# Attention, mixture of experts and a gated feed-forward stage on one core: register loads of the second half's tiles placed later, last-stage weight loads queued at another point

## The chip, the cores and the metric

One core of a Trainium2 chip runs the whole program. The metric is the device time of one execution in microseconds (us). The kernel before took 522.54 us (median of three runs: 522.54, 524.20, 521.99). The trace comes from one more, profiled execution, of 523.88 us.

The engines are TensorE (PE in the profile; its weight loads are PEld), VectorE (DVE), ScalarE (ACT), GpSimd (POOL) and SyncE (SP). SP computes nothing here: it issues most of the DMAs, one after the other. Every engine works through its own list of instructions in order; where an instruction waits, all behind it in that list wait too.

## The reference

```python
x = attention(q, k, v)                    # 2 x 8 heads, 576 rows of 64, rotary embedding, softmax
x = x.transpose(0, 2, 1, 3).reshape(1152, 512)
e = argmax(x @ w_gate + bias[modality])   # one of 8 experts for each token, gate weight = its probability
out[mask_e] = gate * (relu(x[mask_e] @ w1[e]) @ w2[e])      # w1[e] 512 x 1024, w2[e] 1024 x 512
h = out @ w_in                            # 512 x 2048
y = (h * tanh(softplus(h))) @ w_out       # 2048 x 512
```

Everything is float32. A product is made of three passes on TensorE: each operand is split into a rounded high part and the rest (names in `h` and `l`, as `whi` and `wlo`), and high x high, high x low and low x high are added in PSUM.

## The kernel before, in words

**Stages.** Attention takes the first 170 us. Then come the experts: the tokens of each half of the batch are sorted by expert into rows of a scratch tensor in HBM, and the work is cut into tiles of 304 rows of one expert. Four tiles are always done, named (0, 0), (0, 1), (1, 0) and (1, 1): half and number. Any tile beyond these is done in a loop `For_i(0, n_extra)`, whose count `n_extra` is found on the chip; here it is passed without a turn. From 303 us on runs the last stage, the feed-forward part (`h_unit`, `o_unit` and the `g_` functions).

**One tile.** A tile reads its rows (`xrow`), transposes them (L661), and runs 8 groups of 12 matmuls for the first matrix (`f` in `moe_tile`, whi/wlo chunks 0 to 3, two groups a chunk) and 4 groups of 24 for the second (`d`, chunks 4 to 7). Each of the 8 weight chunks of 512 KB is loaded by SP (`wraw`, L590), rounded on ACT (`whi`, L598) and subtracted on POOL (`wlo`, L603; two of them on DVE). The groups' results pass through ACT (`hh`, L718) and DVE (`hl`, L720).

**Routing of half 1.** While tile (0, 0) starts, DVE works out where the tokens of half 1 go: a chain of some forty small instructions in `routing(1)` and `merge_extra`. Matmuls of tile (0, 0) are put between them by `pump`: each DVE step gives a credit from `P["rq"]`, which is spent on matmuls. The chain leaves three things: the table `tbl` with expert and row of tiles (1, 0) and (1, 1), the list `extra` of further tiles, and their number `nxi`. `tile_rows(1)` has SP read `tbl` into registers (`value_load`, L554 and L555). `values_load(nx)` (L1378) has all five engines read `nxi` into a register.

**Weights of the last stage.** Its 16 weight blocks of 1 MB come in as 64-bit words (`wr`, loaded by `dec_load`, L1289) and are turned into float32 by three DVE instructions a block (L1296, L1301, L1306; `decode` runs one of them). There are two `wr` buffers, so block f + 2 can be loaded only when the third instruction of block f is done. `decode` is called by `drive` at every 24th matmul step of the expert stage, and 48 such instructions are spread over expert and last stage; those that are left when the last stage begins are put between its own DVE work.

Of the kernel before, what the change touches and what calls it, by code (L numbers as in the profile page):

```python
# [35 lines left out]
FC2 = F2 // 128  # L36

Q = {'r0': 2.45, 'rd': 2.0, 'tanh': 1.06, 'rec': 1.1, 'hi': 2.2, 'lo': 2.38, 'o': 3.86}
P = {'sd': (3, 4), 'dl': (28, 44), 'qd': (2, 3), 'alt': (0.1, 4), 'd0': 41, 'vl': 9, 'w3': 3, 'rq': (0.45, 0.47, 0.2), 'dec': (8, 8, 8), 'rl': 3, 'ah': 0, 'eps': 0.05, 'slack': 0.1}
K = {'ld': -22.67, 'prep': (-24.92, -22.38, -23.33, -27.14, -20.49, -7.62), 'sc': (-8.42, -3.18, 1.68, 1.67, 2.84, 10.44, 1.99, 8.05, 9.75), 'max': (-2.26, -5.46, -1.21, -1.85, 5.06, 8.41, 4.71, 11.42, 13.72), 'exp': (-3.19, 1.66, 6.32, 3.7, 13.26, 11.14, 14.6, -2.87, 25.74), 'tr': (0.69, 2.1, 2.56, 2.68, 5.53, 7.5, 8.45, 9.85, 10.88, 11.85, 15.56, 16.66, 16.92, 19.98), 'hi': (-3.91, -0.31, 2.51, 3.62, 4.25, 4.9, 5.01, 5.32, 7.26, 9.77, 13.56, 14.12, 14.6, 15.66), 'lo': (0.77, 1.83, 5.61, 6.34, 6.67, 7.32, 10.02, 10.73, 12.18, 13.92, 13.94, 14.62, 17.33, 18.02), 'pv': (7.08, 7.84, 10.5, 10.69, 14.13, 14.25, 14.32, 15.96, 18.04, 20.31, 21.03, 22.86, 23.97, 25.61), 'evac': (14.53, 9.65, 6.27, 25.13), 'rec': (-4.7, -0.45, 4.11, 12.71), 'fmm': (4.53, -3.79, 16.24, 17.22), 'norm': (15.5, 16.11, 26.18, 35.69)}  # L40

QT = [(0, 128), (128, 128), (256, 64), (320, 128), (448, 128)]
# [31 lines left out]
class Plan:  # L74
# [39 lines left out]
    def pick(self, e):  # L114
        best, lines = None, set()
        for o in self.todo[e][:40]:
# [8 lines left out]
            if best is None or t < best[0] - 1e-9:  # L125
                best = (t, o)
            if t <= self.free[e] + P["eps"]:
                break
# [40 lines left out]
    def run(self):  # L169
# [3 lines left out]
        while any(self.todo.values()):  # L173
            best = None
            for e in self.todo:
                c = self.pick(e)
                c = c and (c[0], 1, c[1])
                for o in self.alt[e][:4]:
# [4 lines left out]
                    t = max(t, self.free[e])  # L183
                    if (c is None or t + o[4] - P["alt"][0] <= c[0]) and t + o[4] + P["alt"][1] < end:
                        c = (t, 1, o)
                for st in self.streams:
# [3 lines left out]
                    if st["gate"] and not st["gate"](t):  # L190
                        continue
                    if c is None or t + (st["next"][1] - P["slack"] if e in st["low"] else 0.0) <= c[0]:
                        c = (t, 0, st)
# [19 lines left out]
def moe_kernel(ctx: ExitStack, tc: tile.TileContext, aps, out):  # L213
    nc = tc.nc
    scratch = nc.dram_tensor("scratch", [ROWS, RW], F32).ap()
    extra = nc.dram_tensor("extra", [NS[1] - 2, 2], I32).ap()
# [309 lines left out]
    def merge_extra(nx):  # L526

        V = nc.vector
        n0, n1 = NS[0] - 2, NS[1] - 2
        sh = [1, n0, 2]  # L530
        m = rp.tile([1, n0], F32, tag="mm", name="mm")
        yield "dve", 0.12, True
        V.tensor_scalar(
            out=m, in0=iotat[0:1, 0:n0], scalar1=nxs[0], scalar2=None, op0=ALU.is_lt
        )
        d = rp.tile(sh, F32, tag="md", name="md")
        yield "dve", 0.12, True
        V.tensor_tensor(out=d, in0=tes[0][:, 2:], in1=tms[1][:, 2:2 + n0], op=ALU.subtract)
        yield "dve", 0.12, True
        V.tensor_tensor(out=d, in0=d, in1=m[:, :, None].to_broadcast(sh), op=ALU.mult)  # L540
        yield "dve", 0.12, True
        V.tensor_tensor(
            out=tes[1][:, 2:2 + n0], in0=tms[1][:, 2:2 + n0], in1=d, op=ALU.add
        )
        ei = const.tile([1, n1, 2], I32, name="ei")
        yield "dve", 0.12, True
        V.tensor_copy(ei, tes[1][:, 2:])
        yield "dve", 0.12, True
        V.tensor_tensor(out=nx, in0=nxs[0], in1=nxs[1], op=ALU.add)
        nc.sync.dma_start(out=extra.rearrange("(o r) c -> o r c", o=1), in_=ei)  # L550

    def tile_regs(row):
        return dict(
            e=nc.sync.value_load(row[:, 0:1], min_val=0, max_val=NE - 1),  # L554
            c=nc.sync.value_load(row[:, 1:2], min_val=0, max_val=ROWS - T),  # L555
            y=lambda: nc.scalar.value_load(row[:, 1:2], min_val=0, max_val=ROWS - T),
        )
# [34 lines left out]
    def split_chunk(k, i):  # L592
# [6 lines left out]
        lo = pool.tile([128, 1024], F32R, tag="wlo", name=f"wlo{k}_{i}", bufs=n)  # L599
        dve = k == (0, 0) and i in P["sd"]  # L600
        yield ("dve", 1.14, False) if dve else ("pool", 2.3, False)
# [4 lines left out]
    class Feed:  # L606
# [6 lines left out]
        def loads(self, n):  # L613
            self.want = max(self.want, min(n, len(self.seq)))
            while self.nl < min(self.want, self.ns + (2 if len(wpool) == 1 else P["w3"])):
                k = self.seq[self.nl][0]
# [56 lines left out]
    def moe_tile(k, feed, bank):  # L673

        at_ = feed.tiles.index(k)
        ah = 4 if len(wpool) == 1 else 2 + P["w3"] + P["ah"]
        kk = at_ * NCH
# [516 lines left out]
    cur = {}  # L1194

    def all_tiles(keys):
        for k in keys:
            yield from moe_tile(k, feed, lambda: cur["bank"]())

    gen0 = all_tiles(main[:2])  # L1200
    done0 = []

    def route(b):
        yield from routing(b, lambda: cur["rbank"]())
        if b:
            tile_rows(b)

    def tile_rows(b):
        for i in range(2):
            regs[b, i] = tile_regs(tbl[b][:, i])  # L1210
# [52 lines left out]
    def pump(x):  # L1263

        owed[0] += x
        while owed[0] > 0:
            y = next(gen0, None)
            if y is None:
                done0.append(1)
                return  # L1270
            if y[0] == "pe":
                owed[0] -= y[1]
# [14 lines left out]
    def dec_load(f):  # L1287
        wr[f] = t = wrp.tile([128, 1024, 2], I32, tag="wr", name=f"wr{f}")
        nc.sync.dma_start(out=t.rearrange("p a b -> p (a b)"), in_=aps["wio"][f].bitcast(I32))  # L1289

    def dec(f):


        t = wr.pop(f)
        w = WC[f].bitcast(I32)
        nc.vector.tensor_scalar(  # L1296
            out=w, in0=t[:, :, 1], scalar1=3, scalar2=0x3FFFFFFF,
            op0=ALU.logical_shift_left, op1=ALU.bitwise_and,
        )
        yield  # L1300
        nc.vector.scalar_tensor_tensor(  # L1301
            out=w, in0=t[:, :, 1], scalar=-0x40000000, in1=w,
            op0=ALU.bitwise_and, op1=ALU.bitwise_or,
        )
        yield
        nc.vector.scalar_tensor_tensor(  # L1306
            out=w, in0=t[:, :, 0], scalar=29, in1=w,
            op0=ALU.logical_shift_right, op1=ALU.bitwise_or,
        )
        yield  # L1310

    def dec_all():
        for f in range(FC2):
            d = dec(f)
            next(d)
            yield
            next(d)
            yield
            next(d)
            if f + 2 < FC2:  # L1320
                dec_load(f + 2)
            yield

    dgen = dec_all()
    nd = [0]

    def decode(n, limit=3 * FC2):
        for _ in range(n):
            if nd[0] < limit:
                nd[0] += 1  # L1330
                next(dgen)

    with ExitStack() as mctx:
# [11 lines left out]
        nq_ = [0]  # L1345

        def drive(gen, every, limit=3 * FC2, steps=1000):
            for y in gen:
                if y == "last":
                    break  # L1350
                if y == "quiet":
                    limit = 0
                if y[0] == "y":
                    for i in range(2):
                        split_y(0, i, y[1:])
                if y[0] != "pe":
                    continue
                nq_[0] += 1
                if nq_[0] % (3 * every) == 0:
                    decode(1, limit)  # L1360
                steps -= 1
                if not steps:
                    break
# [3 lines left out]
        for i, y in enumerate(chain(route(1), merge_extra(nx))):  # L1367
            if i in P["dl"]:
                dec_load(len(wr))
            if y[0] == "dve":  # L1370
                pump(P["rq"][(i > 9) + (i > 20)])
        xctx.close()
        lctx = ExitStack()
        for c, n, b in ((sctx, "wp3", P["w3"]), (lctx, "lp", 1)):
# [17 lines left out]
        def split_y(g, i, cs=range(KC)):  # L1392
            c0, n, hs = GR[g]
            o, w = T + c0 + sum(hs[:i]), hs[i]
            if cs[0] == 0:
                yh[g, i] = ypool[g].tile([128, KC, w], F32R, name=f"yh{g}_{i}")
                yl[g, i] = ypool[g].tile([128, KC, w], F32R, name=f"yl{g}_{i}")
            a, b = yh[g, i], yl[g, i]
            for c in cs:
                nc.scalar.activation(out=a[:, c], in_=Y[:, c, o:o + w], func=AF.Copy)  # L1400
                nc.vector.tensor_tensor(  # L1401
                    out=b[:, c], in0=Y[:, c, o:o + w], in1=a[:, c].bitcast(F32), op=ALU.subtract
                )
# [141 lines left out]
        for q in range(nq):  # L1545
# [18 lines left out]
            o = m + Q["o"]  # L1564
# [17 lines left out]
        ps_h = pool("ps_h", 3, space=PSUM)  # L1582
        for i in range(2):
            split_y(0, i, [KC - 1])
        for _, _, fn, a in sorted(ev2, key=lambda e: e[:2]):
            fn(*a)

# [58 lines left out]
```

## Time and profile before

| | |
|---|---|
| median of three runs | 522.54 us |
| profiled execution | 523.88 us, of it 522.2 us from the first to the last instruction |
| PE busy | 480.7 us (92% of the span) |
| DVE, POOL, ACT busy | 409.8, 366.3, 332.4 us |
| mean granted TensorE clock | 0.977 of full speed |

A busy share is a mean over stages that have different limits. To judge one place one looks at the stretch of the span it lies in: what each engine did there, what PE waited for, and which clock it was granted. Matmuls overlap, so the time of one matmul is read from the distance between starts or from a long run of them, not from a single duration.

### The profile page before, as it was taken

To read this page: it belongs to the slowest core of one execution; us is meant where nothing else is said; L and a number is where in the kernel's file an instruction comes from. 1 tells how busy PE (TensorE), PEld (TensorE's weight loads), DVE (VectorE), ACT (ScalarE), POOL (GpSimd) and SP (SyncE) were. 2 spreads that over 40 slices of the span, in tenths; PEclk is the share of its full clock that TensorE was granted. 3 is DMA by queue.
4 is the path that set the end of the run, shared out by engine and by line. 5 is a ranking of instruction groups with operands and counts; after the bars stand their busy time and mean duration, and the time that the engine had idled before them with its cause. 6 is when DMAs were issued, how large, how long until landed. Compare 5 with 4: busy or idle time off the path is not lost.

```text
span 522.2 us, 9092 instructions
## 1 busy us (share of the span) xinstructions
PE 480.7 (92%) x3152; PEld 444.8 (85%) x3152; DVE 409.8 (78%) x586; ACT 332.4 (64%) x750; POOL 366.3 (70%) x359
## 2 busy tenths in 40 slices
PE   2699999999999979898999988899999899999995
PEld 1589999998988869897989987789898789999994
DVE  6489888898887665481696889999999967877773
ACT  2388788767869515454464475666666568776763
POOL 4889989999833355664777665677778558977664
PEclk9999999999999979899999999999999899999998
DMA  6588976777633684683875522022220000100001
GB/s 210 140 193 228 229 204 171 208 185 206 140 122 130 203 313 158 225 310 121 282 247 203 211 82 81 1 81 82 80 82 2 1 2 40 49 14 1 1 1 81
DMA packets 24131, 69.42 MB, mean 133 GB/s; under 512 B 5522, under 2 KB 9810, under 8 KB 22034
## 3 DMA queue, kind: packets, MB, share of 16 engines
q1 hardware_dynamic: 21794, 63.16, 39.9%
q0 software_dynamic: 1456, 5.03, 2.4%
q10 hardware_dynamic: 832, 0.61, 0.4%
q8 instruction: 26, 0.43, 0.3%
q14 instruction: 23, 0.19, 0.1%
HBM read 49.08 MB, written 6.44 MB: 106 GB/s over the span
## 4 chain that ended last, share of the span: by engine, by line
PE 34%; DVE 12%; ACT 2%; issue 2%; POOL 2%; DMA 1%; POOLq 0%; ACTq 0%
PE h L1453 13%; PE o L1510 13%; PE mm L695 7%; DVE ta L1475 6%; DVE wc L1306 1%; DVE wc L1301 1%; DMA wraw(1, 0)_5_3587<-in_w_dram 1%; DVE yl L1401 1%; DVE ta L1476 1%; POOL wlo(1, 0)_2_3552 L603 1%; POOL wlo(1, 0)_1_3542 L603 0%; ACT w2h L1436 0%; PE mm L661 0%; DVE wc L1296 0%; POOL out_dram L1520 0%
## 5 line engine op out<-in xcount | busy, mean ns | idle before, releaser
L1475 DVE RECIPROCAL ta<-ta 128x320 f32<-128x320 f32 (+1 forms) x64 | 124.7, 1948 | 22.0 <-ACT ta L1468 20.7
L1493 POOL TENSOR_TENSOR g<-ta,g 128x320 fp32r<-128x320 f32 (+1 forms) x63 | 60.1, 954 | 61.4 <-issue 29.0
L1510 PE MATMUL o<-w2h,g 128*128 128x512 f32 x288 | 101.0, 398 | 0.0
L1437 POOL TENSOR_TENSOR w2l<-wc,w2h 128x512 fp32r<-128x512 f32 x64 | 85.7, 1360 | 3.5 <-ACT w2h L1436 3.5
L1453 PE MATMUL h<-yh,w2h 128*128 128x320 f32 (+1 forms) x256 | 76.4, 299 | 6.2 <-DVE ta L1476 6.2
L1453 PE MATMUL h<-yh,w2l 128*128 128x320 f32 (+1 forms) x256 | 76.2, 298 | 0.6 <-POOL w2l L1437 0.6
L1453 PE MATMUL h<-yl,w2h 128*128 128x320 f32 (+1 forms) x256 | 75.9, 297 | 0.2 <-DVE yl L1401 0.2
L963 PE MATMUL sc<-sk,sq 128*128 128x288 f32 (+1 forms) x320 | 59.8, 320 | 15.4 <-ACT sk L890 9.4
L984 ACT ACTIVATE pexp<-sc,nm 128x576 f32<-128x576 f32 x72 | 53.3, 741 | 24.2 <-DVE nm L973 19.3
L973 DVE TENSOR_REDUCE nm<-sc 128x1 f32<-128x576 f32 x72 | 53.5, 751 | 14.6 <-PE sc L963 11.0
L1510 PEld LDWEIGHTS o<-w2h,g 128*128 128x128 f32 x288 | 54.5, 190 | 11.0 <-POOL g L1493 1.0
L963 PEld LDWEIGHTS sc<-sk,sq 128*128 128x128 f32 (+1 forms) x320 | 47.6, 195 | 17.7 <-ACT sk L890 9.4
L1017 ACT ACTIVATE ph<-pt 128x512 fp32r<-128x512 f32 (+2 forms) x112 | 54.6, 510 | 12.2 <-PE pt L997 11.6
L1453 PEld LDWEIGHTS h<-yh,w2h 128*128 128x128 f32 x256 | 48.4, 189 | 11.1 <-DVE ta L1476 7.8
L997 PE MATMUL pt<-ident,pexp 128*128 128x128 f32 (+1 forms) x360 | 54.9, 278 | 2.7 <-DVE pl L1023 1.8
L1510 PE MATMUL o<-w2l,g 128*128 128x512 f32 x144 | 57.2, 397 | 0.0
L1487 ACT ACTIVATE g<-ta 128x320 fp32r<-128x320 f32 (+1 forms) x64 | 27.9, 436 | 41.7 <-DVE ta L1476 41.6
L1023 DVE TENSOR_TENSOR pl<-pt,ph 128x512 fp32r<-128x512 f32 (+1 forms) x80 | 48.9, 628 | 3.0 <-ACT ph L1017 2.6
L1038 PE MATMUL av<-ph,vhl 128*128 128x256 f32 (+1 forms) x160 | 50.9, 334 | 0.4 <-ACT avt L1047 0.2
L1453 PEld LDWEIGHTS h<-yl,w2h 128*128 128x128 f32 x256 | 48.3, 189 | 2.6 <-DVE yl L1401 0.4
L1453 PEld LDWEIGHTS h<-yh,w2l 128*128 128x128 f32 x256 | 48.3, 189 | 0.8 <-POOL w2l L1437 0.8
L997 PEld LDWEIGHTS pt<-ident,pexp 128*128 128x128 f32 (+1 forms) x360 | 42.1, 138 | 5.7 <-issue 2.0
(440 smaller groups left out, 1229.5 us busy)
## 6 DMA issues: line engine op xcount, KB each, us to landing
wr<-in_wio_dram SPq DMA_DIRECT2D x16, 1024.0 KB, 4.8
xs<-in_qk_dram SPq DMA_DIRECT2D x15, 576.0 KB, 5.1
sk<-ab SPq DMA_DIRECT2D x30, 288.0 KB, 4.1
sq<-ab SPq DMA_DIRECT2D x30, 144.0 KB, 2.6
vraw<-in_v_dram SPq DMA_DIRECT2D x16, 160.0 KB, 3.9
scratch<-zero SPq DMA_DIRECT2D x12, 108.8 KB, 3.8
xrow(0, 0)_2307<-scratch SPq DMA_DIRECT2D x2, 290.0 KB, 2.9
xrow(0, 1)_2675<-scratch SPq DMA_DIRECT2D x2, 290.0 KB, 4.2
```

The costliest lines, as they stand in the source:

```text
L963: nc.tensor.matmul(t[:m, hf, :NC2], lhsT=sq[:, c:c + m], rhs=sk[:, z, hf * NC2:(hf + 1) * NC2], start=(z == 0), stop=(z == 1),)
L973: nc.vector.tensor_reduce(out=nm[n, j], in_=sc[n, j][:, :, :NC2], axis=AX.XY, op=ALU.max, negate=True)
L984: nc.scalar.activation(out=pe, in_=sc.pop((n, j))[:, :, :NC2], func=AF.Exp, bias=nm.pop((n, j)), accum_out=st[n, hf][:, i:i + 1],)
L997: nc.tensor.transpose(out=t[:kn, o:o + 128], in_=pexp[n, j][:, k0:k0 + kn], identity=ident)
L1017: nc.scalar.activation(out=block(ph, n, hf, kts, slice(0, kn)), in_=psum(n, hf, kts, kn), func=AF.Copy)
L1023: nc.vector.tensor_tensor(out=block(pl, n, hf, kts, slice(0, 128)) if kn == 128 else block(ph, n, hf, kts, slice(64, 128)), in0=psum(n, hf ...
L1038: nc.tensor.matmul(av[n, hf][:, :u.nq], lhsT=vhl[n][:, kt].rearrange("p a d -> p (a d)"), rhs=src[:, kt, u.at:u.at + u.nq], start=(kt == 0 ...
L1437: nc.gpsimd.tensor_tensor(out=lo[:, cs], in0=w[:, cs], in1=hi[:, cs].bitcast(F32), op=ALU.subtract)
L1453: nc.tensor.matmul(ps[:, :w], lhsT=wt[:, c], rhs=m[g, i][:, c], start=(n == 0), stop=(n == 11))
L1475: nc.vector.reciprocal(out=ta, in_=ta)
L1493: eng.tensor_tensor(out=gt[q][1][:, o:o + w], in0=tas.pop((q, i))[:, :w], in1=gt[q][0][:, o:o + w].bitcast(F32), op=ALU.subtract,)
L1510: nc.tensor.matmul(acc[g, t], lhsT=a[:, s], rhs=b, start=(f == 0 and z == 0), stop=(f == FC2 - 1 and z == 2),)
```

## The change

Four things are altered.

- The credits of `pump` go from (0.45, 0.47, 0.2) to (0.52, 0.55, 0.25).
- After the routing chain, 24 further matmul steps of the expert tiles are issued before `tile_rows(1)`, and the DMA of `extra` is issued there too instead of at the end of `merge_extra`.
- After them another 24 steps (9 before) come ahead of `values_load(nx)`.
- `dec_all` no longer issues the next `wr` load right behind the third decoding instruction. It notes it in `due`, and `flush` issues it 16 matmul steps later. From the last stage on it is issued at once, as before.

```diff
-P = {... 'vl': 9, 'w3': 3, 'rq': (0.45, 0.47, 0.2), ...}
+P = {... 'vl': 24, 'w3': 3, 'rq': (0.52, 0.55, 0.25), ...}
...
-        nc.sync.dma_start(out=extra.rearrange("(o r) c -> o r c", o=1), in_=ei)
+        cur["ei"] = ei
...
     def route(b):
         yield from routing(b, lambda: cur["rbank"]())
-        if b:
-            tile_rows(b)
...
+    due, behind = [], [True]
+
+    def flush():
+        while due:
+            dec_load(due.pop(0))
...
             next(d)
             if f + 2 < FC2:
-                dec_load(f + 2)
+                due.append(f + 2)
+                if not behind[0]:
+                    flush()
...
                 if nq_[0] % (3 * every) == 0:
                     decode(1, limit)
+                if nq_[0] % (3 * every) == 2 * every:
+                    flush()
...
             if y[0] == "dve":
                 pump(P["rq"][(i > 9) + (i > 20)])
+        drive(gen0, P["dec"][0], P["d0"], P["vl"])
+        tile_rows(1)
+        nc.sync.dma_start(out=extra.rearrange("(o r) c -> o r c", o=1), in_=cur["ei"])
         xctx.close()
...
         for i in range(2):
             split_y(0, i, [KC - 1])
+        behind[0] = False
+        flush()
```

What this does to the order is seen on three engines. In these rows L1289 is the load of a weight block (L1287 after the change), L590 the load of an expert chunk, L554 and L555 the register loads of a tile.

PE, in tile (0, 0), around the load of `nxi`, before (872 is its place in PE's list):

```order
870 L695 MATMUL mm_2808<-xh(0, 0)_2507,whi(0, 0)_3_2641 128x304
871 L695 MATMUL mm_2808<-xl(0, 0)_2508,whi(0, 0)_3_2641 128x304
872 L1378 TENSOR_LOAD nxi
873 L695 MATMUL mm_2808<-xh(0, 0)_2507,wlo(0, 0)_3_2643 128x304
874 L695 MATMUL mm_2848<-xh(0, 0)_2507,whi(0, 0)_3_2641 128x304
```

And now:

```order
927 L695 MATMUL mm_2900<-hh(0, 0)_2578,whi(0, 0)_5_2752 128x304
928 L695 MATMUL mm_2900<-hl(0, 0)_2579,whi(0, 0)_5_2752 128x304
929 L1389 TENSOR_LOAD nxi
930 L695 MATMUL mm_2900<-hh(0, 0)_2578,wlo(0, 0)_5_2754 128x304
931 L695 MATMUL mm_2900<-hh(0, 0)_2578,whi(0, 0)_5_2752 128x304
```

The load stands 57 places later: then in the matmuls of chunk 3, now near the end of those of chunk 5.

SP, at the fifth chunk of tile (0, 0), before:

```order
132 L581 DMA xrow(0, 1)_2675<-scratch 48x580
133 L1289 DMA wr_2697<-in_wio_dram 128x2048
134 L590 ISA
135 L590 DMA wraw(0, 0)_5_2708<-in_w_dram 128x1024
136 L554 TENSOR_LOAD tbl_2743
137 L554 ISA x2
```

And now:

```order
132 L581 DMA xrow(0, 1)_2671<-scratch 48x580
133 L590 ISA
134 L590 DMA wraw(0, 0)_5_2697<-in_w_dram 128x1024
135 L1287 DMA wr_2716<-in_wio_dram 128x2048
136 L590 ISA
137 L590 DMA wraw(0, 0)_6_2750<-in_w_dram 128x1024
138 L1287 DMA wr_2785<-in_wio_dram 128x2048
```

Chunk 5 now stands ahead of the first weight block, and chunk 6 ahead of the register loads.

SP, at the first chunks of tile (0, 1), before:

```order
152 L590 ISA
153 L590 DMA wraw(0, 1)_0_2908<-in_w_dram 128x1024
154 L1289 DMA wr_2956<-in_wio_dram 128x2048
155 L590 ISA
156 L590 DMA wraw(0, 1)_1_2970<-in_w_dram 128x1024
157 L590 ISA
158 L590 DMA wraw(0, 1)_2_3003<-in_w_dram 128x1024
```

And now:

```order
151 L590 DMA wraw(0, 1)_0_2894<-in_w_dram 128x1024
152 L1389 TENSOR_LOAD nxi
153 L1389 ISA x2
154 L590 ISA
155 L590 DMA wraw(0, 1)_1_2967<-in_w_dram 128x1024
156 L590 ISA
157 L590 DMA wraw(0, 1)_2_3000<-in_w_dram 128x1024
158 L1287 DMA wr_3015<-in_wio_dram 128x2048
```

The third weight block stood ahead of chunks 1 and 2 of tile (0, 1), and now stands behind them. On DVE 24 decoding instructions stood ahead of the first `yl` of the last stage; now 23 do.

## Rows read from the trace of the kernel before

**Rows 1.** Profile page, its first line.

```profile
span 522.2 us, 9092 instructions
```

**Rows 2.** Windows: stretch, length, busy us (instructions) by engine, granted clock, DMA share, GB/s.

```profile
172.40:185.50 13.10, 12.41 (x88) 12.10 (x87) 10.01 (x40) 6.02 (x13) 6.34 (x7) 1.00 0.68 240
185.54:189.42 3.88, 0.17 (x3) 0.03 (x1) 2.80 (x16) 0.50 (x1) 2.12 (x4) 0.82 0.89 350
189.42:194.87 5.45, 5.45 (x21) 5.45 (x22) 1.77 (x4) 1.40 (x3) 2.37 (x1) 0.50 0.63 246
...
213.26:215.32 2.06, 0.17 (x2) 0.00 (x1) 0.75 (x2) 2.06 (x4) 2.06 (x2) 1.00 0.02 8
215.32:218.78 3.46, 3.46 (x14) 3.46 (x15) 1.47 (x3) 0.90 (x2) 3.46 (x2) 0.51 0.58 187
...
242.60:244.84 2.24, 0.17 (x2) 0.00 (x0) 0.00 (x0) 0.56 (x2) 0.00 (x0) 1.00 0.03 7
...
246.20:249.50 3.30, 3.30 (x15) 3.30 (x14) 1.61 (x2) 0.93 (x2) 3.30 (x2) 0.50 0.27 96
249.50:303.00 53.50, 53.15 (x378) 51.98 (x376) 41.71 (x40) 28.90 (x51) 37.27 (x15) 1.00 0.65 228
```

**Rows 3.** Waits of PE, 150 to 345 us: total, times, longest.

```profile
PE mm L695 <- DVE nxi L549: 3.7, 1, 3.7
...
PE mm L695 <- POOL wlo(0, 1)_1_3007 L603: 1.9, 1, 1.9
```

**Rows 4.** Timeline of DVE: start, duration, instruction.

```profile
188.44 0.14 DVE L549 TENSOR_TENSOR nxi<-nx,nx 1x1 int32<-1x1 f32 x1
...
202.47 1.63 DVE L1306 SCALAR_TENSOR_TENSOR wc<-wr,wc 128x1024 int32<-128x1024 int32 x1
...
271.37 2.89 DVE L1296 TENSOR_SCALAR wc<-wr 128x1024 int32<-128x1024 int32 x1
```

**Rows 5.** Line L1378, PE's own register load: ns min/median/max, start.

```profile
L1378 PEldq TENSOR_LOAD <-nxi x1: 739/739/739, 188.6 to 188.6; - x1
```

**Rows 6.** Timeline of SP: DMA issues.

```profile
178.88 0.41 SPq L1289 DMA_DIRECT2D wr<-in_wio_dram  x1
180.77 0.33 SPq L590 DMA_DIRECT2D wraw(0, 0)_5_2708<-in_w_dram  x1
...
190.84 0.33 SPq L590 DMA_DIRECT2D wraw(0, 0)_6_2801<-in_w_dram  x1
...
204.13 0.34 SPq L1289 DMA_DIRECT2D wr<-in_wio_dram  x1
204.68 0.98 SPq L590 DMA_DIRECT2D wraw(0, 1)_1_2970<-in_w_dram  x1
...
262.98 0.34 SPq L1289 DMA_DIRECT2D wr<-in_wio_dram  x1
```

**Rows 7.** DMA issues, 168 to 345 us: size, us from issue to landing.

```profile
wraw(0, 0)_5_2708<-in_w_dram SPq DMA_DIRECT2D x1, 512.0 KB, 8.1
...
wraw(1, 0)_4_3548<-in_w_dram SPq DMA_DIRECT2D x1, 512.0 KB, 3.1
```

**Rows 8.** Tile wr: landing times of all 16 weight blocks.

```profile
DMA to landing us min/median/max: 4.7/4.8/7.5
```

**Rows 9.** Timeline of POOL: end of half 1's scatters, chunk 5.

```profile
187.99 0.09 POOL L418 MEMSET spacer<- 1x1 f32 x1
190.06 2.37 POOL L603 TENSOR_TENSOR wlo(0, 0)_5_2805<-wraw(0, 0)_5_2708,whi(0, 0)_5_2803 128x1024 fp32r<-128x1024 f32 x1 [1.98 <-PE mm L695]
```

**Rows 10.** Timeline of ACT: rounding of chunk 5.

```profile
188.92 1.06 ACT L598 ACTIVATE whi(0, 0)_5_2803<-wraw(0, 0)_5_2708 128x1024 fp32r<-128x1024 f32 x1 [4.27 <-DMA wraw(0, 0)_5_2708<-in_w_dram]
```

**Rows 11.** Chain that ended last, two pieces: start, duration.

```profile
269.35 33.60 PE mm L695 x240
...
402.22 1.94 DVE wc L1301
404.22 1.67 issue
```

**Rows 12.** Line L1306, third decoding instruction: ns min/median/max.

```profile
L1306 DVE SCALAR_TENSOR_TENSOR wc<-wr,wc x16: 1207/1800/2817, 202.5 to 404.2; 128x1024 int32<-128x1024 int32 x16
```

More of the change, by code (lines that the diff above doesn't have):

```diff
@@ L38 @@
 Q = {'r0': 2.45, 'rd': 2.0, 'tanh': 1.06, 'rec': 1.1, 'hi': 2.2, 'lo': 2.38, 'o': 3.86}
-P = {'sd': (3, 4), 'dl': (28, 44), 'qd': (2, 3), 'alt': (0.1, 4), 'd0': 41, 'vl': 9, 'w3': 3, 'rq': (0.45, 0.47, 0.2), 'dec': (8, 8, 8), 'rl': 3, 'ah': 0, 'eps': 0.05, 'slack': 0.1}
+P = {'sd': (3, 4), 'dl': (28, 44), 'qd': (2, 3), 'alt': (0.1, 4), 'd0': 41, 'vl': 24, 'w3': 3, 'rq': (0.52, 0.55, 0.25), 'dec': (8, 8, 8), 'rl': 3, 'ah': 0, 'eps': 0.05, 'slack': 0.1}
 K = {'ld': -22.67, 'prep': (-24.92, -22.38, -23.33, -27.14, -20.49, -7.62), 'sc': (-8.42, -3.18, 1.68, 1.67, 2.84, 10.44, 1.99, 8.05, 9.75), 'max': (-2.26, -5.46, -1.21, -1.85, 5.06, 8.41, 4.71, 11.42, 13.72), 'exp': (-3.19, 1.66, 6.32, 3.7, 13.26, 11.14, 14.6, -2.87, 25.74), 'tr': (0.69, 2.1, 2.56, 2.68, 5.53, 7.5, 8.45, 9.85, 10.88, 11.85, 15.56, 16.66, 16.92, 19.98), 'hi': (-3.91, -0.31, 2.51, 3.62, 4.25, 4.9, 5.01, 5.32, 7.26, 9.77, 13.56, 14.12, 14.6, 15.66), 'lo': (0.77, 1.83, 5.61, 6.34, 6.67, 7.32, 10.02, 10.73, 12.18, 13.92, 13.94, 14.62, 17.33, 18.02), 'pv': (7.08, 7.84, 10.5, 10.69, 14.13, 14.25, 14.32, 15.96, 18.04, 20.31, 21.03, 22.86, 23.97, 25.61), 'evac': (14.53, 9.65, 6.27, 25.13), 'rec': (-4.7, -0.45, 4.11, 12.71), 'fmm': (4.53, -3.79, 16.24, 17.22), 'norm': (15.5, 16.11, 26.18, 35.69)}
```

## The prediction

> **What bounds the kernel now.** I read the windows first, then PE's waits, then the lists of the engines PE waited for, and last the chain. From attention to the last stage the matmuls set the pace, but not evenly. The windows [rows 2] show three places in the expert stage where PE all but stops: 3.88 us from 185.54, 2.06 us from 213.26 and 2.24 us from 242.60. After each the granted clock is 0.50 or 0.51, which is the lower of its two levels, for 5.45, 3.46 and 3.30 us. I call the places A, B and C. Between them PE has little idle time: from 249.50 to 303.00 it is busy for 53.15 of 53.50 us. The chain [rows 11] goes through PE there, with 240 matmuls in 33.60 us, 0.140 us each; that is my price of a matmul at the full clock. So what A and B lose reaches the start of the last stage undiminished, and so would what is saved there. In the last stage DVE is on the chain about 402 us, with decoding instructions in it [rows 11].
>
> What A and B are is told by the waits [rows 3]. At A a matmul waits for `nxi`. The matmul does not read it: the register load standing in PE's list does, and everything behind it stops. `nxi` is made at 188.44 and is ready at 188.58 [rows 4], the load takes 0.739 us from then [rows 5], and PE goes on at 189.42. At B PE waits for the low part of chunk 1 of tile (0, 1). That chunk was issued only at 204.68, right behind a weight-block load at 204.13 [rows 6], and that one had to wait for the third decoding instruction of block 0, 202.47 to 204.10 [rows 4]. SP stood there since the chunk before, and chunk 1 stood behind it.
>
> C is the passing of the loop of further tiles. The change leaves it.
>
> **The change part by part.**
>
> *Register load, place A.* The load moves 57 products later in PE's list. PE would reach it at 185.54 + 57 x 0.140 = 193.5, some 4.9 us after 188.58. The routing chain itself may end up to half a microsecond later, since more results of tile (0, 0) now stand within it. So the wait for `nxi` goes, 3.88 us. The slow stretch goes with it: 21 matmuls in 5.45 us [rows 2] would take 21 x 0.140 = 2.94, so 2.51 us more. A is worth 6.39 us. The load itself still has to run, now with no wait ahead of it. Bounds: 0, if PE has matmuls queued enough to cover it, and 0.74 us, its whole duration [rows 5]. I take 0.74, because at A the matmuls went on only after it. A hold of that length should not lower the clock: from 172.40 to 185.50 PE was idle for 13.10 - 12.41 = 0.69 us and the granted clock stayed at 1.00 [rows 2].
>
> *What is late next at A.* PE then reaches chunk 5 (second group of the second matrix) after the last product of group 6, 12 of group 7 and 24 of the first: 185.54 + 37 x 0.140 = 190.7. POOL can start on `wlo` of chunk 5 when the scatters of half 1 are out, 188.08 before and perhaps 0.5 us later now, and needs 2.37 us [rows 9]: 190.5 to 191.0. The two meet within 0.3 us, if ACT has rounded the chunk by then. Before, it had not: the chunk was issued at 180.77 [rows 6], took 8.1 us [rows 7] and ACT was done at 188.92 + 1.06 = 189.98 [rows 10]. Left so, `wlo` would come at 189.98 + 2.37 = 192.4, and PE would wait 1.7 us. But the 1 MB weight block issued 1.9 us ahead of it [rows 6] now stands behind it, and with less in its way a chunk lands in as little as 3.1 us [rows 7]. I take a landing by 186 and no wait; the bound above is 1.7 us and a slow stretch as at B.
>
> Two transfers issued so close could also just share the bandwidth, and then their order changes nothing. The Trainium skill, in "DMA: Bandwidth & Descriptors", section "Queues, rings and completion order", says that each DMA engine consumes one queue's descriptors in ring order and takes turns only between queues. By that the move past the weight block counts and the scatters, on GpSimd's queue, still take their turns; with plain sharing chunk 5 would keep its 8.1 us. The 8.1 against 3.1 us fit either. By the rule the sum stays as it is; without it, it is the first rival below.
>
> *Chunks 6 and 7.* Chunk 6 was issued at 190.84 [rows 6], behind SP's register loads. It now stands ahead of them and can go when chunk 4's buffer is free, some 5 us earlier; its matmuls, which then begin near 196, have it in time.
>
> *Weight block behind the chunks, place B.* Chunks 1 and 2 of tile (0, 1) now stand ahead of the block that held SP. They go when SP has done its register loads, near 195, instead of at 204.68. PE reaches chunk 1 near 213.26 - 6.39 + 0.74 = 207.6 with A gone. Issue, 8.1 us of landing at the worst, 1.06 on ACT and 2.37 on POOL make 206.5: in time. B goes: 2.06 us, and 14 matmuls in 3.46 us instead of 14 x 0.140 = 1.96, another 1.50 us. Together 3.56 us.
>
> *Later loads of blocks.* Each is asked for 16 products (2.24 us) later. The shortest gap between an issue and the use was 271.37 - 262.98 = 8.39 us [rows 4, 6]; less 2.24 it is 6.15, above the median landing of 4.8 us and below the longest of 7.5 [rows 8]. So I cost it at nothing, hidden by DVE's other work; uncovered it is a rival.
>
> *One decoding instruction fewer before the last stage.* 23 instead of 24 stand ahead of it, so DVE has one more in a stage in which it is on the chain. Its price is between 0 (hidden where PE is ahead) and 2.82 us, the longest of the third kind [rows 12]. I take 1.5, between the shortest, 1.21, and the median, 1.80.
>
> *Sum.* -6.39 - 3.56 + 0.74 + 1.50 = -7.71 us. The profiled execution took 523.88 us: its span of 522.2 [rows 1] and 1.68 around it. The sum makes it 516.2. The runs' median lies 1.34 us below the profiled time, so I forecast 522.54 - 7.71 = 514.8.
>
> **The rivals.**
>
> 1. *Chunk 5 takes the place of A.* For it: POOL and PE meet within 0.3 us at best, and DMA was at 0.89 of its capacity in that stretch [rows 2]. Against: chunk 5 is now the first in its queue. It gives back 1.7 + 1.5 us: 518.0.
> 2. *B stays.* SP now has the register loads and `extra` ahead of chunk 1. For it: these loads wait for the end of routing. Against: they have some 8 us in hand. Then 514.8 + 3.56 = 518.4.
> 3. *The load still waits.* If the longer routing chain makes `nxi` as late as the load, A only moves, and the saving at B pays for the extra decoding: 522.54 - 3.56 + 1.50 + 0.74 = 521.2. Against it stand 4.9 us of room.
> 4. *Slower: blocks that come late.* If the DMA queue is fuller once PE no longer stops, a block's data may land after DVE asks for it. DVE's `hl` stand behind that, and PE behind them. It decides where landing exceeds the gap of 6.15 us. At 7.5 us each block costs 1.35 us, and if each stop also lowers the clock as at B, 1.5 more. With six blocks loaded between the tiles that is 17 us: 514.8 + 17 = 532. For it: the shortest gap fails against the longest landing. Against: five of six gaps would have to fall to that one's size.
>
> **How the numbers follow.** Forecast 0.68, rival 1 0.13, rival 2 0.08, rival 3 0.06, rival 4 0.05. A measurement of this kernel can tell about 0.5%, 2.6 us, from no change: faster means under 519.9, slower over 525.2. The forecast and the first two rivals are faster, 0.89, less 0.02 for cases in which two of them meet: 0.87. Rival 3 and those make same 0.08, rival 4 slower 0.05. The lower end leaves out both added costs, 522.54 - 9.95 = 512.6, and also the slow stretch after C, 3.30 - 15 x 0.140 = 1.2 us: 511.4. The upper end takes rivals 1 and 2 and stops before rival 3 is whole: 520.0. The forecast's own range is 512.6 to 516.
>
> **What would show it.** In the profile after: PE's waits name neither `nxi` nor `wlo(0, 1)_1`; the windows at A and B show the full clock; the register load is 0.74 us near 193; chunk 5 lands before 186; the loop is reached near 233 us and the last stage begins near 294 instead of 303; one decoding instruction more lies in it. I am wrong if PE waits over 1 us on chunk 5 or 7, if DVE idles ahead of L1294, or if the last stage lasts over 2 us longer than before.

## The result, and the profile after

The changed kernel took 516.31 us (median of four runs: 512.77, 516.95, 517.50, 515.67), and the kernel before 522.26 us beside it. The ratio is 0.9877, 95% interval [0.983, 0.9923]. In a second set of runs on one chip it took 514.68 us against 522.64, ratio 0.9841 [0.9798, 0.9885]. The change makes the kernel 1.2 to 1.6% faster. The forecast, 514.8, lies between the two medians. A kernel's runs that lie more than 1.5% above its fastest, a slower state, are left out of the medians and ratios in this text; that concerns three runs of the kernel before and five of the run with a decoding at every 18th step.

The trace after is of the run of 512.77 us, the shortest of the four, so single differences between the two traces are to be weighed, not only added up.

```profile
span 511.1 us, 9097 instructions
```

The windows of after come in the columns of [rows 2]: stretch, length, busy us and instructions of PE, PEld, DVE, ACT and POOL, granted clock, DMA share, GB/s. The first is tile (0, 0) up to where A was, then A's place, B's place and the passing of the loop (C).

```profile
170.63:185.50 14.87, 14.13 (x101) 13.88 (x101) 11.59 (x46) 7.07 (x13) 8.10 (x12) 1.00 0.68 218
185.50:190.00 4.50, 4.19 (x30) 3.95 (x29) 4.29 (x14) 1.05 (x3) 2.03 (x1) 1.00 1.03 423
190.00:215.00 25.00, 25.00 (x177) 24.11 (x176) 14.00 (x18) 14.93 (x26) 20.28 (x8) 1.00 0.79 276
...
230.95:233.02 2.07, 0.00 (x1) 0.00 (x1) 0.00 (x0) 0.56 (x2) 0.00 (x0) 1.00 0.03 8
...
234.34:237.70 3.36, 3.36 (x15) 3.36 (x15) 1.65 (x2) 0.97 (x2) 3.36 (x2) 0.53 0.31 101
```

From 185.50 to 215.00 PE is idle for 0.31 us, and the granted clock is 1.00 throughout. The stops of 3.88 and 2.06 us in [rows 2] and the slow stretches behind them are gone. C is there as before: 2.07 us without work and, 1.3 us after it, 15 matmuls at 0.53.

The waits of PE, 150 to 345 us (total, times, longest), answer to [rows 3]. Neither `nxi` nor `wlo(0, 1)_1` is among them; the largest of the expert stage is C.

```profile
PE h L1464 <- DVE ta L1487: 3.7, 3, 1.6
PE mm L695 <- issue: 2.1, 1, 2.1
...
PE mm L695 <- DVE hl(0, 0)_2579 L720: 0.3, 1, 0.3
```

SP's list after, against [rows 6]: chunk 5 goes 0.39 us ahead of the first block instead of 1.89 behind it, and chunks 1 and 2 of tile (0, 1) go at 195.13 and 195.68, ahead of the third block at 199.46.

```profile
178.51 0.34 SPq L590 DMA_DIRECT2D wraw(0, 0)_5_2697<-in_w_dram  x1
178.90 0.42 SPq L1287 DMA_DIRECT2D wr<-in_wio_dram  x1
181.75 0.33 SPq L590 DMA_DIRECT2D wraw(0, 0)_6_2750<-in_w_dram  x1
...
195.13 0.33 SPq L590 DMA_DIRECT2D wraw(0, 1)_1_2967<-in_w_dram  x1
195.68 0.33 SPq L590 DMA_DIRECT2D wraw(0, 1)_2_3000<-in_w_dram  x1
199.46 0.34 SPq L1287 DMA_DIRECT2D wr<-in_wio_dram  x1
```

ACT rounds chunk 5 without a wait ahead of it, where it had stood 4.27 us for the data in [rows 10]:

```profile
182.79 1.06 ACT L598 ACTIVATE whi(0, 0)_5_2752<-wraw(0, 0)_5_2697 128x1024 fp32r<-128x1024 f32 x1
```

POOL starts on it at 185.12 instead of 190.06 [rows 9]:

```profile
185.12 2.40 POOL L603 TENSOR_TENSOR wlo(0, 0)_5_2754<-wraw(0, 0)_5_2697,whi(0, 0)_5_2752 128x1024 fp32r<-128x1024 f32 x1
```

PE's register load, the row that answers to [rows 5]:

```profile
L1389 PEldq TENSOR_LOAD <-nxi x1: 490/490/490, 189.8 to 189.8; - x1
```

It runs from 189.8 to 190.3. In PE's list only four matmuls stand between it and the transposes (L661) of tile (0, 1), and these begin at 192.84; its place among the matmuls is thus 192.84 - 4 x 0.14 = 192.3. The load ran 2 us ahead of its place, while PE worked on what stood before it, and PE shows no idle time there. So PE's list is not worked strictly one instruction after the other, as the opening has it for every engine: a register load whose value is ready goes ahead of matmuls that stand before it.

**The stages.** I measure from the first expert matmul to the last `Y` on the chain of tile (1, 1), and from there to the last `ot`:

| | first expert matmul | last `Y` | last `ot` | expert stage | last stage |
|---|---|---|---|---|---|
| before | 172.44 | 302.97 | 513.11 | 130.53 | 210.14 |
| after | 170.63 | 290.60 | 502.04 | 119.97 | 211.44 |
| after, second set | 172.32 | 292.42 | 503.85 | 120.10 | 211.43 |

The expert stage gives 10.56 us, the last one takes 1.30 back. The other 1.81 us of this pair of traces lie ahead of the first expert matmul, where the change does nothing; over all traces of this study that matmul starts between 170.6 and 173.8, and the two traces of after alone differ by 1.69. The start goes with the granted clock early in attention, from 20 to 35 us. These are before and after from 25 to 30 us:

```profile
25.00:30.00 5.00, 4.24 (x25) 3.83 (x24) 2.15 (x3) 2.04 (x5) 4.75 (x5) 0.74 0.88 243
25.00:30.00 5.00, 3.81 (x30) 3.35 (x28) 3.15 (x6) 3.05 (x8) 4.75 (x5) 1.00 0.87 239
```

Of all eleven traces only two keep 1.00 throughout these 15 us, and only these two begin the expert stage before 172: the first of after (170.63) and that of the run with 25 decoding instructions (171.40).

**The last stage.** The chain that ended last (start, duration, instruction) in after, from DVE's hands to PE's:

```profile
326.47 2.00 DVE wc L1299
...
383.18 1.95 DVE wc L1299
...
392.70 1.93 DVE wc L1299
...
399.08 2.03 PE h L1464 x12
401.10 1.40 PE o L1521 x6
```

And the same in before (L1301 there is L1299 here, L1453 is L1464):

```profile
338.33 0.50 DVE ta L1476
...
338.96 2.00 PE h L1453 x12
...
408.61 2.51 PE h L1453 x12
411.11 2.46 PE o L1510 x6
```

In before, DVE has caught up by 338.96 and the chain goes over to PE for 33 us. In after it stays with DVE from 295 to 399 us: there is one decoding instruction more, and DVE never gets ahead. From the last `Y` to where PE takes over for good it is 408.61 - 302.97 = 105.64 us before and 399.08 - 290.60 = 108.48 after. The extra instruction costs 2.84 us. That the whole stage is only 1.30 longer is a slow stretch: behind 408.61 the two pieces of before took 4.97 us and those of after 3.43, so before's execution lost 1.54 there.

### The profile page after: what moved, and what is told of

Same layout as the page of the kernel before. It is cut to its first block, busy times and chain, and to the rows that moved or that the text cites. A ratio compares the mean times of both kernels' runs of the same rounds, so it can differ in the third digit from the quotient of the medians.

```text
span 511.1 us, 9097 instructions
## 1 busy us (share of the span) xinstructions
PE 473.7 (93%) x3152; PEld 437.3 (86%) x3152; DVE 406.4 (80%) x586; ACT 331.5 (65%) x750; POOL 368.8 (72%) x359
## 4 chain that ended last, share of the span: by engine, by line
PE 32%; DVE 18%; issue 3%; ACT 1%; POOL 0%; POOLq 0%
DVE ta L1486 11%; PE mm L695 11%; PE h L1464 10%; PE o L1521 10%; DVE wc L1299 2%; DVE ta L1487 1%; DVE yl L1412 1%; DVE wc L1294 1%; DVE wc L1304 1%; PE mm L661 0%; POOL out_dram L1531 0%; POOLq L1655 0%; DVE idi L1599 0%; ACT ot L1527 0%; ACT ta L1479 0%
## 5 line engine op out<-in xcount | busy, mean ns | idle before, releaser
L1504 POOL TENSOR_TENSOR g<-ta,g 128x320 fp32r<-128x320 f32 (+1 forms) x63 | 57.7, 916 | 62.0 <-issue 31.5
L1448 POOL TENSOR_TENSOR w2l<-wc,w2h 128x512 fp32r<-128x512 f32 x64 | 88.9, 1411 | 3.4 <-ACT w2h L1447 3.4
L1464 PE MATMUL h<-yh,w2h 128*128 128x320 f32 (+1 forms) x256 | 76.5, 299 | 6.7 <-DVE ta L1487 6.7
L1464 PE MATMUL h<-yh,w2l 128*128 128x320 f32 (+1 forms) x256 | 75.9, 297 | 0.6 <-POOL w2l L1448 0.6
L1464 PE MATMUL h<-yl,w2h 128*128 128x320 f32 (+1 forms) x256 | 75.8, 296 | 0.2 <-DVE yl L1412 0.2
L963 PE MATMUL sc<-sk,sq 128*128 128x288 f32 (+1 forms) x320 | 58.3, 314 | 15.6 <-ACT sk L890 9.3
L963 PEld LDWEIGHTS sc<-sk,sq 128*128 128x128 f32 (+1 forms) x320 | 46.4, 190 | 17.5 <-ACT sk L890 9.3
L1464 PEld LDWEIGHTS h<-yh,w2h 128*128 128x128 f32 x256 | 48.2, 188 | 11.9 <-DVE ta L1487 9.1
L1464 PEld LDWEIGHTS h<-yl,w2h 128*128 128x128 f32 x256 | 48.1, 188 | 2.6 <-DVE yl L1412 0.4
L1464 PEld LDWEIGHTS h<-yh,w2l 128*128 128x128 f32 x256 | 48.2, 188 | 0.8 <-POOL w2l L1448 0.8
```

What stands on the lines that cost most here:

```text
L963: nc.tensor.matmul(t[:m, hf, :NC2], lhsT=sq[:, c:c + m], rhs=sk[:, z, hf * NC2:(hf + 1) * NC2], start=(z == 0), stop=(z == 1),)
L1448: nc.gpsimd.tensor_tensor(out=lo[:, cs], in0=w[:, cs], in1=hi[:, cs].bitcast(F32), op=ALU.subtract)
L1464: nc.tensor.matmul(ps[:, :w], lhsT=wt[:, c], rhs=m[g, i][:, c], start=(n == 0), stop=(n == 11))
L1504: eng.tensor_tensor(out=gt[q][1][:, o:o + w], in0=tas.pop((q, i))[:, :w], in1=gt[q][0][:, o:o + w].bitcast(F32), op=ALU.subtract,)
```

## The experiments

Runs `r_after` to `c_24_decodings` were made together, then the next three, then the last two. Each set has its own runs of the kernel before (medians 522.64, 522.06 and 522.17 us).

**The changed kernel again** (no edit).

> The changed kernel once more, beside the parts. Both theories: 6 to 8 us below the kernel before, some 515 us. In its trace PE's waits name neither nxi nor chunk 1 of tile (0, 1). If the 1.8 us by which the first profile of it was ahead already at the first expert matmul came from the change, they are there again (first expert matmul near 170.7); if they came from a clock that happened not to fall near 25 us, a profile in which it falls has that matmul near 172.4.

Measured: 514.68 us (six runs, 512.16 to 516.29), ratio 0.9841 [0.9798, 0.9885]. The stages stand in the table above and agree with the first trace within 0.13 us. The expectation's question is answered too: the clock fell near 25 us (0.77 from 25 to 30), and the first expert matmul came at 172.32. Chunk 5 was issued at 180.18 here, and ACT waited 0.60 us for it, starting at 185.13; PE waited for `hl(0, 0)` for 0.31 us, as in the first trace.

**Only the register loads later**: the credits, the further steps and the place of the loads as in after, the blocks asked for at once.

```diff
-    due, behind = [], [True]
+    due, behind = [], [False]
```

> The register loads and the list moved and the credits raised as in the change, but each weight block is asked for right behind the decoding that frees its buffer, as before. Theory 1 (two separate stalls): only place A goes, 6.4 us, and the extra decoding in the last stage costs 1.5 to 3, so 4 to 5 us below before, about 518; SP still stands at a block, now ahead of chunk 2 of tile (0, 1). Theory 2 (moving the register loads also frees the chunks, the later asking for blocks does nothing): same as the whole change, about 515 to 516, and no wait of PE at tile (0, 1).

Measured: 517.56 us, ratio 0.9909 [0.9875, 0.9944]; expert stage 122.24 us. Its longest wait of PE besides C:

```profile
PE mm L695 <- DVE hl(0, 1)_3036 L720: 1.2, 1, 1.2
```

And SP's list of this run:

```profile
198.22 0.33 SPq L590 DMA_DIRECT2D wraw(0, 1)_1_2967<-in_w_dram  x1
202.46 0.34 SPq L1287 DMA_DIRECT2D wr<-in_wio_dram  x1
203.01 0.33 SPq L590 DMA_DIRECT2D wraw(0, 1)_2_3002<-in_w_dram  x1
```

A is gone without the other part of the change. B has only moved and shrunk: the block, still behind its decoding, now holds chunk 2 instead of chunk 1, because the new credits shifted decoding against products (`decode` counts the steps of `drive`, not those of `pump`); PE waits 0.61 us for `wlo(0, 1)_2` at 212.03 and 1.22 for `hl(0, 1)`. These two stops, with the full clock behind both, make 1.83 of the 2.27 us that this expert stage is longer than that of after. The first theory forecast about 518 and a block ahead of chunk 2, and so it came.

**Only the blocks apart**: the kernel before with `due`, `flush` and `behind`, and nothing else of the change.

```diff
...
             if f + 2 < FC2:
-                dec_load(f + 2)
+                due.append(f + 2)
+                if not behind[0]:
+                    flush()
...
+                if nq_[0] % (3 * every) == 2 * every:
+                    flush()
...
```

> The kernel before with only the other part: blocks are asked for 16 matmul steps after the decoding. Theory 1: place A stays with its 3.9 us and slow stretch, place B goes, 3.6 us, and 24 decodings still stand ahead of the last stage: 518.5 to 519. Theory 2: the block still stands ahead of chunk 2, so PE waits there instead of at chunk 1 and nothing is gained: 521.5 to 522.5.

Measured: 518.66 us, ratio 0.9912 [0.9874, 0.995]; expert stage 124.96 us, last stage 210.15. The wait of A stays, and of the expert stage's waits only C's comes next, with 2.1 us; that of B is gone:

```profile
PE mm L695 <- DVE nxi L549: 3.7, 1, 3.7
```

SP now issues chunk 1 ten microseconds ahead of the block:

```profile
194.94 0.33 SPq L590 DMA_DIRECT2D wraw(0, 1)_1_2968<-in_w_dram  x1
205.18 0.34 SPq L1289 DMA_DIRECT2D wr<-in_wio_dram  x1
```

Chunk 2 still stands behind the block (205.80), but PE doesn't wait for it. So each part takes away its own stop, and 518.66 lies in the range of the first theory. The stage is 5.57 us shorter, more than B's 3.56; about 1 us of it is A, whose slow stretch was milder in this execution (18 matmuls in 4.00 us against 21 in 5.45); the last 1 us I can't place. Since the first part also shrinks B, the gains of the two alone (8.29 and 5.57 us of the expert stage) add up to more than the 10.56 of both.

**One decoding instruction back ahead of the last stage**: the count of steps begins at 12, so 24 instead of 23 stand ahead.

```diff
-        nq_ = [0]
+        nq_ = [12]
```

> The changed kernel with the count of matmul steps begun at 12, so that decodings come 12 steps earlier and 24 instead of 23 stand ahead of the last stage. Theory 1: the last stage gets back the one decoding on DVE's chain, 1.5 to 3 us below the changed kernel. Theory 2: that one was hidden beside TensorE and the last stage lasts as long: within 0.5 us of the changed kernel.

Measured: 512.78 us, ratio 0.9833 [0.9789, 0.9877], against 514.68 of after in the same set. Expert stage 119.53, last stage 208.57, which is 2.87 less than after. The chain goes over to PE early again, as before the change:

```profile
327.76 2.00 PE h L1464 x12
...
397.39 2.02 PE h L1464 x12
```

397.39 lies 105.61 us behind its last `Y` (291.78), where before had 105.64. That settles the price of the extra instruction. In the expert stage a remainder of B is back: the block at 201.57 stands ahead of chunk 2 at 202.13, and PE waits 0.5 us for `wlo(0, 1)_2`. Asking 16 steps later does not by itself put the chunks first; it depends on where decoding stands.

**The first block ahead of chunk 5 again**: its load is asked for at step 24 of the routing chain instead of step 28, the rest is as in after.

```diff
-P = {... 'dl': (28, 44), ...}
+P = {... 'dl': (24, 44), ...}
```

> The changed kernel with its first weight block asked for ahead of chunk 5 of tile (0, 0) again, as before the change; all else as changed. If the order on SP decides (theory 1), chunk 5 lands some 8 us after its issue instead of about 4 and ACT ends its rounding near 188 instead of 184, its subtraction comes near 190.5, and PE, which needs it near 189, waits 1 to 2 us: 1 to 3.5 us above the changed kernel. If the transfers only share the bandwidth (theory 2), chunk 5 lands as in the changed kernel and the time is the same within 0.5 us.

Measured: 520.29 us, ratio 0.995 [0.9913, 0.9987]; expert stage 124.41 us. SP, ACT and PE of this run:

```profile
178.91 0.41 SPq L1287 DMA_DIRECT2D wr<-in_wio_dram  x1
180.36 0.33 SPq L590 DMA_DIRECT2D wraw(0, 0)_5_2699<-in_w_dram  x1
```

```profile
188.83 1.06 ACT L598 ACTIVATE whi(0, 0)_5_2752<-wraw(0, 0)_5_2699 128x1024 fp32r<-128x1024 f32 x1 [4.03 <-DMA wraw(0, 0)_5_2699<-in_w_dram]
189.80 0.72 ACT L718 ACTIVATE hh(0, 0)_2578<-mm 128x304 fp32r<-128x304 f32 x2
```

```profile
195.17 0.62 PE L695 MATMUL mm<-hl(0, 0)_2579,whi(0, 0)_4_2701 128*128 128x304 f32 x1 [3.73 <-DVE hl(0, 0)_2579 L720]
```

Behind the block, chunk 5 is there 8.5 us after its issue; in after's second trace, issued at almost the same time (180.18) but ahead of the block, it is there after 4.95 (185.13). Over all traces ACT starts on the chunk 7.5 to 8.5 us after its issue where the block stands ahead (three traces), and 4.3 to 5.6 us after it where the block stands behind, with one exception in eight: 7.2 us in the run with every 21st step. So the order counts: had the two only shared the bandwidth, it would have changed nothing, as the prediction put it. The Trainium skill, "DMA: Bandwidth & Descriptors", section "Queues, rings and completion order", says that one queue's descriptors are consumed in ring order; the two runs agree.

What PE then waits for is not the chunk, but `hl`, for 3.73 us, nearly the length of A's stop, with a granted clock of 0.70 over the 5.33 us behind. ACT stands 4.03 us at the rounding, and the results of the first matrix's last groups (`hh`) queue behind it until 189.80. The last `hl` then stands on DVE behind two routing instructions that took 1.55 and 2.08 us. These are they, then POOL's subtractions in the same run, then the two instructions in after:

```profile
190.81 1.55 DVE L540 TENSOR_TENSOR md<-md,mm 1x16 f32<-1x16 f32 x1
...
192.59 2.08 DVE L547 CAST ei<-te 1x32 int32<-1x32 f32 x1
```

```profile
189.97 2.36 POOL L603 TENSOR_TENSOR wlo(0, 0)_5_2754<-wraw(0, 0)_5_2699,whi(0, 0)_5_2752 128x1024 fp32r<-128x1024 f32 x1 [2.97 <-ACT whi(0, 0)_5_2752 L598]
192.29 2.34 POOL L603 TENSOR_TENSOR wlo(0, 0)_6_2807<-wraw(0, 0)_6_2750,whi(0, 0)_6_2805 128x1024 fp32r<-128x1024 f32 x1
```

```profile
188.04 0.16 DVE L540 TENSOR_TENSOR md<-md,mm 1x16 f32<-1x16 f32 x1
...
188.44 0.17 DVE L547 CAST ei<-te 1x32 int32<-1x32 f32 x1
```

The two are 3.30 us longer than in after, most of the 3.73, and each ends 0.03 to 0.04 us behind a subtraction on POOL (192.33 and 194.63). This is no accident of one run: in all nine traces with the raised credits one of three routing instructions (L533, L540, L547) is stretched to 1.55 us or more and ends at most 0.04 us behind POOL's subtraction of chunk 5. So the late chunk delays POOL, POOL's work then falls on the end of the routing chain, and `hl` comes after that. Why these instructions last until POOL is done, and their neighbours don't, no run here shows.

Most of the gain is lost (ratio 0.995 against 0.9841), 4.44 us of it in the expert stage. I had expected 1 to 3.5 us over the changed kernel; the medians are 5.6 apart. So moving the register load without the order of chunk 5 and the block mostly exchanges A's stop for another of nearly its length.

**Decoding faster**, every 21st step instead of every 24th, and every 18th.

```diff
-P = {... 'dec': (8, 8, 8), ...}
+P = {... 'dec': (7, 7, 7), ...}
```

> The changed kernel with a decoding at every 21st matmul step instead of every 24th, which puts 26 of the 48 ahead of the last stage (23 in the changed kernel, 24 in the kernel before). If decoding on DVE's chain sets the last stage's first 100 us, each one that goes is worth 1 to 3 us until TensorE alone bounds: last stage 4 to 6 us shorter than in the changed kernel, about 510. Rival: weight blocks asked for more often come late or stand ahead of chunks again; then the expert stage grows by 2 us or more and eats it.

> The same with a decoding at every 18th step: 31 ahead of the last stage. If decoding alone bounds there, up to 8 us below the changed kernel; TensorE is idle for about 8 us in that stretch, so no more than that: 507 to 509. Rival: blocks every 54 steps fill the DMA queue (1 MB in 7.6 us beside 512 KB in each 3.4 us), PE waits on chunks in the expert stage and the time is no better than at every 21st.

Measured for every 21st: 512.73 us, ratio 0.9799 [0.9749, 0.985]; expert stage 123.53, last stage 207.52. With 26 decoding instructions ahead the last stage is 3.9 us shorter than after's, but PE waits for `hl` of both tiles of half 0 (1.4 and 1.2 us) and the expert stage is 3.6 longer. For every 18th (31 ahead): 517.13 us, ratio 0.9915 [0.9864, 0.9967], where 507 to 509 had been expected. Its waits of PE:

```profile
PE h L1464 <- DVE yl L1412: 4.3, 1, 4.3
...
PE mm L695 <- DVE hl(0, 1)_3037 L720: 2.6, 1, 2.6
```

For every 21st step the rival on record was right that the expert stage grows by over 2 us. Its cause, a block ahead of a chunk, came only in small: the block at 203.34 stands ahead of chunk 2 of tile (0, 1) at 203.90, and PE waits 0.5 us for it. The two waits for `hl` are more, and they differ. That for `hl(0, 1)` lies behind a decoding instruction on DVE:

```profile
220.92 2.65 DVE L1304 SCALAR_TENSOR_TENSOR wc<-wr,wc 128x1024 int32<-128x1024 int32 x1
```

That for `hl(0, 0)` does not: no decoding instruction stands ahead of it (the first begins at 192.44). There chunk 5 was rounded only at 188.12, 7.2 us after its issue though it stood ahead of the block, and L540 took 1.57 us, as in the run with the block in front. With every 18th step DVE has no room in half 1 either: from 249 to 303 us it is busy for 53.60 of 54.00 us, and PE waits for `yl` at the start of the last stage.

**Faster only in half 1.** Every 24th step in half 0, every 21st in half 1: 25 ahead.

```diff
-P = {... 'dec': (8, 8, 8), ...}
+P = {... 'dec': (8, 7, 7), ...}
```

> The kernel after, with a decoding instruction at every 21st step only from tile (1, 0) on; the tiles of half 0 keep every 24th. That brings 25 instead of 23 decoding instructions ahead of the last stage. Theory (a decoding instruction that falls into the last stage costs its chain about its own time, some 1.4 to 1.9 us, and the waits for hl that every 21st step brought lay in the tiles of half 0, where weight chunks, routing and decoding share DVE): no new wait for hl in half 0, the expert stage as after (120 us), the last stage shorter by 2 to 4 us, so 511 to 513. Rival (DVE has no room at every 21st step anywhere): new waits for hl in tiles (1, 0) and (1, 1), each with a slow stretch, expert stage 122 to 124 us, and 514 to 516.

Measured: 510.63 us (509.08 to 513.38), ratio 0.9782 [0.9739, 0.9824]. Its longest waits of PE, 170 to 291 us:

```profile
PE mm L695 <- issue: 2.1, 1, 2.1
...
PE mm L695 <- DVE hl(0, 0)_2579 L720: 0.3, 1, 0.3
```

Expert stage 120.0 us as in after, with no new wait in the expert stage; last stage 207.24, 4.2 us less than after's 211.44 for two instructions fewer, a little more than the 2 to 4 expected. The first of the two is worth 2.87 (the run with 24), the second 1.33, and a third nothing more (207.52 with 26 ahead). The median is the lowest of all kernels here.

The same with the count begun at 12:

> As the run before, and the count of steps begins at 12 as in the run with 24 decoding instructions: again 25 ahead of the last stage, each at another step. Theory: the same saving in the last stage, 510 to 513, and no new wait of PE. Rival (the place of each decoding instruction between the hl decides, not how many there are): the two runs differ by over 2 us, with a wait for hl in the slower one only.

Measured: 511.56 us, ratio 0.9799 [0.9751, 0.9848]; expert stage 120.1, last stage 207.55. The two cannot be told apart: within what these runs can tell, the number ahead of the last stage counts, not the step at which each stands.

## Why the prediction was right

- *A and B.* Both waits and both slow stretches went, and each part alone took away the one it was said to: A with the register load moved, B with the blocks apart. Summed at 9.95 us; the expert stage gave 10.56. In windows over the whole stage PE is idle 5.60 us less (8.71 before, 3.11 after) and busy 5.00 less (121.89 and 116.89). The idle time is that of A and B in [rows 2], 3.71 and 1.89, as a few matmuls ran within the two stops of 3.88 and 2.06. The busy time fell by 0.99 more than the 4.01 put for the slow stretches; that I can't place.
- *Rivals 1 to 3.* None came in the changed kernel. The first, in its effect, is what the run with the block in front shows, at more than its price; the second shows in small where the blocks are asked for at once (0.61 us on chunk 2); against the third, `nxi` was made by 188.67 (188.44 + 0.14 in [rows 4], 188.53 + 0.14 here), 1.1 us ahead of its load at 189.8 and 3.6 ahead of the load's place at 192.3, where 4.9 had been forecast.
- *The register load.* I took the upper bound, 0.74, and it cost 0, the lower one. It took 0.49 us and ran some 2 us ahead of its place.
- *What is late next at A.* No wait, as forecast: chunk 5 is there before ACT comes to it at 182.79. The reason given, the order in SP's queue, is shown by the run with the block put in front. But the way a late chunk would hurt was misread: I had PE wait for POOL's `wlo`, 1.7 us; it waited for `hl`, 3.73 us, which ACT's queue held up first and then, for most of it, two routing instructions that lasted until POOL was done.
- *Chunks 6 and 7.* Chunk 6 went at 181.75, 9 us earlier than before instead of some 5, and PE waits for neither, as forecast.
- *Weight block behind the chunks.* Chunk 1 of tile (0, 1) went at 195.13, said to be near 195. PE has no wait there.
- *Later loads of blocks.* Costed at nothing, and they cost PE nothing. But DVE did stand for a block once in the first trace of after, which the prediction had named as a sign of being wrong:

```profile
220.15 1.81 DVE L1294 TENSOR_SCALAR wc<-wr 128x1024 int32<-128x1024 int32 x1 [1.01 <-DMA wr<-in_wio_dram]
```

That block was issued at 212.37, 6.77 us before DVE was free for it, and was there after 7.78; before, the same gap was 13.44 us. So it shrank by far more than the 2.24 us reckoned with. In the second trace of after DVE has no such wait, and PE none behind it in either: the fourth rival's mechanism came, its price didn't. What hurts when DVE is loaded more is `hl` behind decoding, as the runs with more frequent decoding show.

- *One decoding instruction fewer before the last stage.* This is the term that was wrong in size: 1.5 forecast, 2.84 measured, just over the upper bound of 2.82. Without the slow stretch that before happened to have, the last stage would so be over 2 us longer, the other sign of being wrong that was named; as it ran, it was 1.30. I took a price between hidden and whole, though the chain of before already ran through DVE for the first 36 us of the stage and again from 374 us on; one more instruction kept it there for the whole 104.
- *Sum.* The traces give -10.56 + 2.84 = -7.72 for what the change does; the forecast was -7.71. The agreement is two errors that cancel: the load and the expert stage came out 1.35 us better (0.74 + 0.61), the decoding 1.34 worse. The medians fell by 5.95 and 7.96 us.

## What to carry to other kernels

A register load in an engine's list is a wait for everything behind it; put it where its value is long made, and it can cost nothing. In one issuing queue, a transfer that must wait for a buffer belongs behind those that needn't, and the one needed first belongs in front: its order was worth 4.4 us of expert stage here. Work that fills an engine's gaps is free until a later stage runs through that engine; there a leftover piece can cost its whole length and more (2.84 us for the first here, 1.33 for the next, nothing for a third), so count the pieces left over after a reordering. And a late transfer is paid for where its successors on other engines then fall, which need not be where its data is used.

## What was not expected of the hardware

The same stop lowers the clock in one execution and not in another. Before's last stage and that of the run with 24 decoding instructions ahead have the same instructions in the same order at the place where PE takes over. These are their windows, first the stop and then 20 matmuls. Before:

```profile
404.22:408.61 4.39, 2.62 (x12) 1.53 (x10) 4.36 (x4) 0.03 (x1) 0.67 (x1) 1.00 0.00 0
408.61:413.57 4.96, 4.96 (x20) 4.44 (x21) 4.54 (x3) 4.37 (x10) 4.20 (x4) 0.66 0.00 2
```

With 24 decoding instructions ahead:

```profile
393.01:397.39 4.38, 2.49 (x11) 1.41 (x10) 4.34 (x4) 0.02 (x1) 0.66 (x1) 1.00 0.01 4
397.39:400.81 3.42, 3.42 (x20) 3.15 (x21) 2.99 (x3) 3.36 (x8) 2.84 (x3) 1.00 0.00 0
```

PE is idle for 1.8 to 1.9 of 4.4 us in both; the clock is 0.66 behind the one and 1.00 behind the other, 1.54 us apart. (0.66 is a mean: from 411.10 to 412.00 it is 0.50, the lower of the two levels.) The stop of 4.38 or 4.39 us at this place is in seven traces. Behind it the 20 matmuls took 4.96 or 4.97 us at 0.66 in four: before, the runs with only one part of the change, and that with the block in front. They took 3.42 us at 1.00 in three: both of after and the run with 24. At C too, after fell to 0.53 behind its stop (15 matmuls in 3.36 us), and the run with 24 kept 1.00 (30 in 4.23). Such a draw is worth 1.3 us at C and 1.5 us in the last stage; what decides it no run here shows. Together with the 3 us by which the first expert matmul moves with the clock early in attention, these draws are of the size of the scatter between runs of one kernel (512.16 to 516.29 us of after). A single pair of traces, 11.1 us apart here, can therefore not stand for the medians, and a slow stretch behind a stop is a likely price, not a sure one.
